# A planned attention and MLP kernel: chunk 1 of the first four heads is loaded ahead of the first two v blocks

## The chip, the core and the metric

The kernel runs on one core of a Trainium2 chip. The core has five instruction queues that run side by side and wait for each other through semaphores: TensorE (PE in the profile; its weight loads are shown apart as PEld), VectorE (DVE), ScalarE (ACT), GpSimd (POOL) and SyncE (SP). Sixteen DMA engines move data between HBM and the on-chip memories; a transfer is issued by an instruction on POOL, SP or ACT. The metric is the device time of one launch in microseconds (us). Four runs of the kernel before gave 226.29 to 227.66 us with a median of 226.47 us.

## The reference

Two layers follow each other. The first is windowed attention with sinks, for 4 sequences (b), 8 heads (h), 768 tokens, head size 64: a token sees the 128 tokens up to itself and the first 4 tokens of its sequence.

```python
scores = scale * np.matmul(q, k.transpose(0, 1, 3, 2))
keep = is_sink | in_window          # is_sink: pos < 4; in_window: 0 <= rel < 128
scores = np.where(keep, scores, -1000000000.0)
a = np.exp(scores - max); a = a / sum
attn = np.matmul(a, v)
```

The second layer takes the heads side by side as rows x of 512 numbers:

```python
xn = (x - mu) / np.sqrt(var + 1e-06) * g_ln
out = x + np.maximum(xn @ w_ch1, 0.0) @ w_ch2    # w_ch1 512x2048, w_ch2 2048x512
```

Inputs and output are float32; the kernel computes in bf16 with float32 sums.

## The kernel before, in words

**Tiles.** The 3072 tokens are 24 tiles of 128 tokens, six for each sequence. For a tile t = 6b + r, `scores` (line 567 adds a mask by a matmul with the identity for the first three tiles, line 571 is the product k times q) writes into one of two double PSUM buffers, "wide", and ACT takes the exponential (line 582). Scores of a tile come in two halves of four heads each. `values` (lines 631, 638 and 641) multiplies with v and, in a 65th column of ones, sums; then DVE divides and normalises in a chain of five instructions: reciprocal (663), multiply into xt (665), statistics (671, 674) and xn (679). The first ten tiles' xn is turned on PE (718) and copied back into xnt on ACT or DVE (copies have line 222 on ACT and 224 on DVE). `up` (742) multiplies xnt with w_ch1, ACT or DVE apply the maximum (751, 753), `down` (782) multiplies with w_ch2, DVE adds x (795) and SP stores.

**q and k.** They must have the head size on the partitions. For sequence 0 the tokens are loaded in two chunks of 384: `load_first` loads chunk 0 of heads 0 to 3 as float32 through ACT's and SP's queues and casts it on ACT and DVE; `load_runs` loads the rest through POOL with a cast on the way (192 KB each for four heads: chunk 0 of heads 4 to 7, chunk 1 of heads 0 to 3, chunk 1 of heads 4 to 7). `prep_runs` turns a chunk of two heads at a time, a "pair" (12 matmuls at line 454), and copies the result into qkt. Scores of tile 2 need both chunks, as does everything behind them; tiles 0 and 1 need chunk 0 alone. `load_v` (404) loads one block of 128 tokens of v, `load_w` (417, 420) a quarter of a weight matrix (512 KB). `sinks` prepares the four sink tokens: `sel` (303) picks them out of v by a matmul (517), `hmask` and `smask` mask them, line 530 multiplies them with q, line 535 takes the exponential into `es`.

**The order of the work** is written out by a planner, `Plan.emit`. Each piece is an `op` with a cost for an engine that can do it, the ops that it depends on, and a key; the planner walks through an estimated time line and puts the ready op with the lowest key next. Loads on POOL keep the order in which they are declared; each has an estimate, `took`, of how long its data takes after those in front of it. Up to the time `HOLD[0]` (line 46) the planner may keep an engine idle for up to `HOLD[1]` us when an op with a lower key becomes ready soon. Where it expects PE idle during the first 26 us it puts in matmuls on a constant (`spin`, line 236), whose results nobody reads. Only the order that comes out, and the real waits for data and buffers, are in the program; the estimates are not.

Of the kernel before, what the change touches and what calls it, by code (L numbers as in the profile page):

```python
# [11 lines left out]
ALU = mybir.AluOpType  # L12
# [19 lines left out]
class Plan:  # L32
# [10 lines left out]
    WARM = 26.0  # L43
    AHEAD = 2.5
    EARLY = 16.0
    HOLD = 22.0, 0.5

    def __init__(self, spin):
        self.ops, self.spin = [], spin
# [1 line left out]
    def op(self, engs, fn, deps=(), key=0.0, alloc=(), uses=(), lat=0.0):  # L51
        o = Op(engs, fn, deps, key, alloc, uses)
        o.lat = lat
        self.ops.append(o)
        return o

    def emit(self):
# [54 lines left out]
        while waiting:  # L112
# [21 lines left out]
            s, e, o, c = min((x for x in cand if x[1] == e0 and x[0] <= lim), key=lambda x: (x[2].key, x[0]))  # L134
            if s < self.HOLD[0]:

                s, e, o, c = min((x for x in cand if x[1] == e0 and (x[2] is o or x[2].key < o.key - 0.05 and
                                  x[0] < min(s + c - 0.12, s + self.HOLD[1]))), key=lambda x: (x[2].key, x[0]))
            if e == "PE" and s < self.WARM and 7 not in tenant:
# [24 lines left out]
def kernel(  # L164
# [12 lines left out]
    nc = tc.nc  # L177

    B, H, S, D = q.shape
    NS = int(n_sink)  # L180
# [7 lines left out]
    HP = H // 2  # L188
# [31 lines left out]
    def copy(e, dst, src):  # L220
        if e == "ACT":
            nc.scalar.copy(dst, src)
        else:
            ENG[e].tensor_copy(dst, src)
# [14 lines left out]
    op = plan.op  # L239
# [21 lines left out]
    spinner = consts.tile([128, 128], BF16)  # L261
# [3 lines left out]
    sel = consts.tile([128, 128], BF16)  # L265
# [24 lines left out]
    def const_negs(_):  # L290
        nc.vector.tensor_scalar(neg1, mask1, 30000.0, -30000.0, op0=ALU.mult, op1=ALU.add)
        for m1, m0, keep in ((neg1, neg0, 0.0), (mask1, mask0, 1.0)):
            nc.vector.tensor_copy(m0, m1)
            nc.vector.memset(m0[0:NS, :], keep)

    def const_sinks(_):

        nc.gpsimd.affine_select(out=hmask[:, 0:1], in_=spinner[:, 0:1], compare_op=ALU.is_ge,
                                fill=0.0, base=63, pattern=[[0, 1]], channel_multiplier=-1)
        nc.gpsimd.affine_select(out=hmask[:, 1:2], in_=spinner[:, 0:1], compare_op=ALU.is_ge,  # L300
                                fill=0.0, base=-64, pattern=[[0, 1]], channel_multiplier=1)

        nc.gpsimd.affine_select(out=sel, in_=spinner, compare_op=ALU.is_equal, fill=0.0, base=0,
                                pattern=[[0, 32], [-1, NS]], channel_multiplier=1)

        nc.gpsimd.affine_select(out=smask, in_=spinner[:, 0:H], compare_op=ALU.is_ge, fill=0.0, base=0,
                                pattern=[[-32, HP], [-4, 2]], channel_multiplier=1)
        nc.gpsimd.affine_select(out=smask, in_=smask, compare_op=ALU.is_ge, fill=0.0, base=NS - 1,
                                pattern=[[32, HP], [4, 2]], channel_multiplier=-1)
# [5 lines left out]
    begun = op({"POOL": 0.7}, None, key=-1000)  # L315
    ones_done = op({"DVE": 2.0}, None, key=-1000)
    ident_done = op({"POOL": 0.35}, const_ident, [begun], -500)
    half_masks = op({"POOL": 0.6}, const_masks, [begun], -499.5)
    masks_done = neg_done = op({"DVE": 1.3}, const_negs, [half_masks], -700)
    sinks_done = op({"POOL": 1.4}, const_sinks, [begun], -440)  # L320

# [4 lines left out]
    def load(cost, took, go, key, deps=(), alloc=(), uses=()):  # L328
        o = op({"POOL": cost}, go, [begun, issued[-1], landed[-QUEUE]] + list(deps), key, alloc, uses)
        issued.append(o)  # L330
        landed.append(op({"DMA": took}, None, [o], key))
        return landed[-1]
# [7 lines left out]
    def qn_buf(b, x):  # L340
        if (b, x) in qn:
            return []
        qn[(b, x)] = Buf("qkn", 4)
        return [qn[(b, x)]]

    def load_runs(b, c, x, h0, h1, took, key):
        alloc = qn_buf(b, x)
        qb = qn[(b, x)]
        w = S // CHUNKS[b]

        def go(_):
            if qb.t is None:
                qb.t = qkn.tile([128, H * S * D // 128], BF16, name="qkn")
            dst = qb.t.rearrange("p (c h m) -> p c h m", c=CHUNKS[b], h=H)
            nc.gpsimd.dma_start(dst[:, c, h0:h1], (q, k)[x][b, h0:h1, c * w:(c + 1) * w, :]
                                .rearrange("h (p r) d -> p h (r d)", p=128))

        o = load(0.9 if h1 - h0 == H else 0.77, took, go, key, (), alloc, [qb])
        for h in range(h0, h1):
            loaded[(b, c, x, h)] = o  # L360

    def load_first(x, hp, lands, key):

        alloc = qn_buf(0, x)
        qb, raw = qn[(0, x)], Buf("ot", 3) if x else Buf("xnt", 3)
        w = S // CHUNKS[0]

        def go(_):
            if x:
                raw.t = opool.tile([128, DM], FP32, name="ot")  # L370
            else:
                raw.t = xtpool.tile([128, NDM, 512], BF16, name="xnt").rearrange("p j c -> p (j c)").bitcast(FP32)
            (nc.scalar, nc.sync)[x].dma_start(raw.t[:, 0:w].rearrange("p (h m) -> p h m", h=2),
                                      (q, k)[x][0, 2 * hp:2 * hp + 2, 0:w, :].rearrange("h (p r) d -> p h (r d)", p=128))

        def cast(e):
            if qb.t is None:
                qb.t = qkn.tile([128, H * S * D // 128], BF16, name="qkn")
            copy(e, qb.t[:, w * hp:w * (hp + 1)], raw.t[:, 0:w])

        op({"SP": 0.1}, go, [], key, [raw])
        o = op({"XD": 0.1}, None, [], key, lat=lands - 0.8)
        o = op({"ACT": 0.49, "DVE": 0.45}, cast, [o], -600, alloc, [raw, qb])
        for h in (2 * hp, 2 * hp + 1):
            loaded[(0, 0, x, h)] = o
# [16 lines left out]
    def load_v(b, r, key, deps=(), took=0.85):  # L402
        def go(_):
            nc.gpsimd.dma_start(vn_buf[b % 2][:, r, :, 0:D],  # L404
                                v[b, :, 128 * r:128 * (r + 1), :].rearrange("h p d -> p h d"))

        before = [vread[(b - 2, i)] for i in (r, r + 1) if (b - 2, i) in vread] + [vs_done.get(b - 2)]
        vcast[(b, r)] = load(0.9, took, go, key, list(deps) + before)
# [2 lines left out]
    w2s = consts.tile([128, NH1, DM], BF16)  # L411
    w_in = {}

    def load_w(which, c, key):
        def go(_):
            if which == 1:
                nc.gpsimd.dma_start(w1s[:, :, 512 * c:512 * (c + 1)],
                                    moe_w_ch1.rearrange("(j p) c -> p j c", p=128)[:, :, 512 * c:512 * (c + 1)])
            else:
                nc.gpsimd.dma_start(w2s[:, 4 * c:4 * (c + 1), :],  # L420
                                    moe_w_ch2.rearrange("(t p) n -> p t n", p=128)[:, 4 * c:4 * (c + 1), :])

        w_in[(which, c)] = load(0.85, 2.57, go, key)


    prepped, kqb, turns = {}, {}, {}
# [393 lines left out]
        nc.tensor.matmul(gp.t, lhsT=ones, rhs=grow, start=True, stop=True)  # L820

    for x in range(2):
        load_runs(0, 0, x, HP, H, (2.2, 1.1)[x], -499)
    for n, (x, hp) in enumerate((x, hp) for hp in range(2) for x in (1, 0)):
        load_first(x, hp, (3.3, 3.5, 4.6, 4.6)[n], -1000 + n)
    op({"SP": 0.1}, lambda _: nc.sync.dma_start(grow, moe_g_ln.rearrange("(o d) -> o d", o=1)), [], -900)
    for r in range(2):
        load_v(0, r, -496 + r, took=1.4)
    for half in range(2):
        for x in range(2):  # L830
            load_runs(0, 1, x, 4 * half, 4 * half + 4, ((1.5, 1.0), (1.8, 0.6))[half][x], -490 + 2 * half + x)
    for c in range(4):
        load_w(1, c, -470 + 2 * c)
        load_v(0, 2 + c, -469 + 2 * c)
    for c in range(3):
        load_w(2, c, -440 + c)
    for x in range(2):
        load_runs(1, 0, x, 0, H, 3.85, -436 + x)
    load_w(2, 3, -434)
    for r in range(RB):  # L840
        load_v(1, r, -430 + r)
# [94 lines left out]
```

## Time and profile before

The profiled execution took 226.39 us, of which the span from the first to the last instruction is 224.7 us.

| part of the span | what it holds | PE busy |
|---|---|---|
| 0 to 5 us | loads, constants, 30 spins | 3.38 of 5.00 |
| 5 to 10 us | chunk 0 turned, first scores | 5.00 of 5.00 (13 spins and more within) |
| 10 to 15 us | scores and values of tiles 0 and 1 | 4.90 of 5.00 |
| 15 to 21.3 us | chunk 1 turned, tiles 0 and 1 normalised, scores of tile 2 | 5.50 of 6.30 |
| 21.3 to 200 us | `up`, `down`, the other tiles | all but 0.35 us |

The transfers on POOL's queue land in the order of their issue. "Lands" is the issue's start plus the time to landing of that issue:

| transfer | issued at | to landing | lands at |
|---|---|---|---|
| chunk 0, heads 4-7, q | 1.89 | 5.9 | 7.8 |
| chunk 0, heads 4-7, k | 2.90 | 5.9 | 8.8 |
| v block 0 | 3.64 | 6.0 | 9.6 |
| chunk 1, heads 0-3, q | 5.38 | 6.2 | 11.6 |
| chunk 1, heads 0-3, k | 6.12 | 6.4 | 12.5 |
| chunk 1, heads 4-7, q | 6.85 | 6.8 | 13.7 |
| chunk 1, heads 4-7, k | 7.58 | 7.3 | 14.9 |
| w_ch1, first quarter | 8.31 | 8.9 | 17.2 |
| v block 2 | 9.10 | 9.0 | 18.1 |
| w_ch1, second quarter | 11.30 | 9.3 | 20.6 |
| w_ch1, third quarter | 12.95 | 11.1 | 24.1 |
| w_ch1, last quarter | 14.56 | 12.9 | 27.5 |

In the timeline an instruction stands with its start, its duration, engine, line, operation, output and input, and a count; in square brackets is the time that its engine was idle before it, and what ended that. In the chain of work that ended last each line is a start, a duration, an engine and a line. PE's matmuls overlap by a little: the time from start to start is what one costs.

### The profile page before, as it was taken

How to read it: one execution, taken by the hardware profiler on the slowest of the kernel's cores; microseconds unless marked ns; L12 is line 12 of the kernel's file. 1: busy time of each engine (PE TensorE's matmuls, PEld its weight loads, DVE VectorE, ACT ScalarE, POOL GpSimd, SP SyncE). 2: the span in 40 equal slices, each digit the busy share in tenths (PEclk: the TensorE clock that was granted, in tenths of full speed). 3: DMA queues.
4: the chain of work that ended last, by engine and by line, in shares of the span. 5: the costliest groups of instructions: out<-in, count | busy, mean ns of one | idle time of the engine just before them, and what ended most of it. 6: DMA issues, size and time to landing. Idle time of an engine off the chain costs nothing.

```text
span 224.7 us, 4469 instructions
## 1 busy us (share of the span) xinstructions
PE 218.6 (97%) x1835; PEld 123.6 (55%) x1835; DVE 114.9 (51%) x217; ACT 111.1 (49%) x158; POOL 82.4 (37%) x111
## 2 busy tenths in 40 slices
PE   7999999999999999999999999999999999999994
PEld 6465888985545455455454444544454554444852
DVE  4565868044977879589574467470026750021011
ACT  3678775677432585870327762246613157400620
POOL 8978776668520699450733000220006020000000
PEclk9999999999999999999999999999999999999999
DMA  6999999999999599999799011230012130012102
GB/s 164 163 195 196 192 207 204 204 157 155 134 124 254 135 150 139 145 139 181 92 172 240 7 25 47 81 108 0 0 36 85 47 96 1 0 47 93 50 0 93
DMA packets 84774, 25.59 MB, mean 114 GB/s; under 512 B 74385, under 2 KB 81809, under 8 KB 84754
## 3 DMA queue, kind: packets, MB, share of 16 engines
q0 software_dynamic: 59392, 13.24, 69.2%
q1 hardware_dynamic: 24818, 11.67, 26.0%
q10 hardware_dynamic: 544, 0.39, 0.5%
q8 instruction: 14, 0.23, 0.4%
q14 instruction: 6, 0.05, 0.1%
HBM read 27.27 MB, written 6.29 MB: 149 GB/s over the span
## 4 chain that ended last, share of the span: by engine, by line
PE 91%; DVE 4%; DMA 2%; ACT 1%; issue 1%; DVEq 0%
PE single L782 38%; PE single L742 36%; PE wide L571 5%; PE wide L638 3%; PE wide L641 2%; DMA xnt<-in_q_dram 2%; PE wide L631 2%; PE wide L567 1%; PE wide L454 1%; PE single L718 1%; DVE st L671 1%; DVE xt L665 1%; PE single L236 1%; DVE xn L679 1%; PE single L454 1%
## 5 line engine op out<-in xcount | busy, mean ns | idle before, releaser
L742 PE MATMUL single<-xnt,w1s 128*128 128x256 bf16 (+1 forms) x512 | 87.9, 326 | 0.0
L742 PEld LDWEIGHTS <-w1s 128*128 128x128 bf16 x512 | 48.4, 98 | 32.6 <-issue 1.9
L582 ACT ACTIVATE e<-wide 128x1024 bf16<-128x1024 f32 x44 | 43.6, 1023 | 43.4 <-PE wide L571 40.9
L782 PE MATMUL single<-w2s,h1t 128*128 128x512 bf16 x256 | 58.1, 379 | 0.0
L795 DVE SCALAR_TENSOR_TENSOR ot<-single,rs,xt 128x512 f32<-128x512 f32 (+2 forms) x25 | 18.2, 728 | 60.3 <-PE single L782 45.1
L751 ACT ACTIVATE h1t<-single 128x512 bf16<-128x512 f32 x60 | 35.8, 597 | 20.9 <-PE single L742 20.9
L782 PEld LDWEIGHTS <-h1t 128*128 128x128 bf16 x256 | 24.0, 98 | 28.2 <-issue 1.1
L782 PE MATMUL single<-w2s,h1n 128*128 128x512 bf16 (+2 forms) x144 | 30.2, 356 | 0.0
L751 ACT ACTIVATE h1n<-single 128x512 bf16<-128x512 f32 x30 | 17.9, 597 | 22.4 <-PE single L742 22.2
L594 POOL TENSOR_SCALAR_AFFINE_SELECT e<-e 128x512 bf16<-128x512 bf16 (+1 forms) x10 | 7.1, 706 | 46.3 <-ACT e L582 46.3
L691 POOL TENSOR_SCALAR ve<-mv 128x2 f32<-128x2 f32 (+1 forms) x8 | 5.7, 708 | 48.0 <-DVE mv L674 48.0
L404 POOL DMA_DIRECT2D vn<-in_v_dram x24 | 21.7, 920 | 0.0
L592 DVE TENSOR_TENSOR e<-e,mask 128x1024 bf16<-128x1024 bf16 x22 | 15.9, 722 | 9.5 <-ACT e L582 9.3
L782 PEld LDWEIGHTS <-h1n 128*128 128x128 bf16 x144 | 12.6, 98 | 12.3 <-issue 1.3
L679 DVE SCALAR_TENSOR_TENSOR xn<-xt,mv,gb 128x512 bf16<-128x512 bf16 x24 | 18.3, 768 | 0.8
L671 DVE BATCH_NORM_STATS2 st<-xt 128x6 f32<-128x512 bf16 x24 | 16.7, 694 | 0.8
L665 DVE TENSOR_TENSOR xt<-wide,rc 128x512 bf16<-128x512 f32 x24 | 16.6, 691 | 0.8
L638 PE MATMUL wide<-vn,e 128*128 128x65 bf16 x192 | 15.8, 193 | 0.1
L638 PEld LDWEIGHTS <-e 128*128 128x128 bf16 x192 | 13.7, 97 | 2.6 <-issue 0.2
L571 PE MATMUL wide<-qkt 64*128 64x256 bf16 (+1 forms) x192 | 14.5, 263 | 0.0
L641 PE MATMUL wide<-vn,e 128*128 128x65 bf16 x160 | 14.2, 193 | 0.0
L571 PEld LDWEIGHTS <-qkt 64*128 64x128 bf16 x192 | 6.8, 94 | 10.3 <-issue 8.9
(66 smaller groups left out, 165.6 us busy)
## 6 DMA issues: line engine op xcount, KB each, us to landing
out_dram<-ot SPq DMA_DIRECT2D x23, 256.0 KB, 2.2
vn<-in_v_dram POOLq DMA_DIRECT2D x24, 128.0 KB, 8.1
w1s<-in_moe_w_ch_dram POOLq DMA_DIRECT2D x4, 512.0 KB, 10.2
w2s<-in_moe_w_ch_dram POOLq DMA_DIRECT2D x4, 512.0 KB, 13.3
qkn<-in_q_dram POOLq DMA_DIRECT2D x12, 128.0 KB, 8.4
qkn<-in_k_dram POOLq DMA_DIRECT2D x12, 128.0 KB, 8.2
qkn<-in_q_dram POOLq DMA_DIRECT2D x1, 768.0 KB, 14.8
qkn<-in_k_dram POOLq DMA_DIRECT2D x1, 768.0 KB, 17.9
```

The lines of the kernel that those rows point to most:

```text
L404: nc.gpsimd.dma_start(vn_buf[b % 2][:, r, :, 0:D], v[b, :, 128 * r:128 * (r + 1), :].rearrange("h p d -> p h d"))
L571: nc.tensor.matmul(pb.t[:, h2, i], lhsT=kb.t[64 * h2:64 * (h2 + 1), 1, hp, 128 * r:128 * (r + 1)], rhs=kb.t[64 * h2:64 * (h2 + 1), 0, hp, ...
L582: nc.scalar.activation(eb.t, pb.t, AF.Exp, scale=scale)
L638: nc.tensor.matmul(pv[:, half, hh, :], lhsT=weights_of(t, half, i, h2, 0), rhs=vn[:, r, h, 0:D + 1], start=fresh and hh == 0, stop=(r == 0 ...
L641: nc.tensor.matmul(pv[:, half, hh, :], lhsT=weights_of(t - 1, half, i, h2, 128), rhs=vn[:, r - 1, h, 0:D + 1], start=False, stop=True, ski ...
L665: nc.vector.tensor_tensor(xb[t].t.rearrange("p (a h) d -> p a h d", a=2), pv[:, :, :, 0:D], rc[0].unsqueeze(3).to_broadcast([128, 2, 4, D] ...
L671: nc.vector.bn_stats(st, xf)
L679: nc.vector.scalar_tensor_tensor(xnb[t].t, in0=xf, scalar=mvb[g][:, ti, 0:1], in1=gb, op0=ALU.subtract, op1=ALU.mult)
L742: nc.tensor.matmul(pb.t[:, n * i:n * (i + 1)], lhsT=w1s[:, j, 128 * (h0 + i):128 * (h0 + i + 1)], rhs=xtb[g].t[:, j, 0:n], start=(j == 0), ...
L751: nc.scalar.activation(hb.t, pb.t, AF.Relu)
L782: nc.tensor.matmul(pb.t[:, 0:n], lhsT=hidden(g, ht, ti), rhs=w2s[:, ht, c0:c1], start=(ht == 0), stop=(ht == NH1 - 1))
L795: nc.vector.scalar_tensor_tensor(ob.t[:, 0:n], in0=pb.t[:, 0:n], scalar=rsb[g][:, ti:ti + 1], in1=xb[t].t.rearrange("p h d -> p (h d)")[:, ...
```

## The change

Three things are edited. (1) The loads on POOL are declared in another order: chunk 1 of heads 0 to 3 (q, k) now stands ahead of v blocks 0 and 1, not behind them. (2) The mask `sel` is taken out of `const_sinks` into an op of its own with an early key, which puts it ahead of the first load on POOL; the other four selects keep the late key. (3) The planner gets other numbers: `HOLD[0]` is 14 and not 22, and the landing estimates of the loads up to the first quarter of w_ch1 are new.

```diff
-    HOLD = 22.0, 0.5
+    HOLD = 14.0, 0.5
...
+    def const_sel(_):
+
+        nc.gpsimd.affine_select(out=sel, in_=spinner, compare_op=ALU.is_equal, fill=0.0, base=0,
+                                pattern=[[0, 32], [-1, NS]], channel_multiplier=1)
+
     def const_sinks(_):
...
-        nc.gpsimd.affine_select(out=sel, in_=spinner, compare_op=ALU.is_equal, fill=0.0, base=0,
-                                pattern=[[0, 32], [-1, NS]], channel_multiplier=1)
...
-    sinks_done = op({"POOL": 1.4}, const_sinks, [begun], -440)
+    op({"POOL": 0.5}, const_sel, [begun], -499.4)
+    sinks_done = op({"POOL": 0.9}, const_sinks, [begun], -440)
...
-    def load_w(which, c, key):
+    def load_w(which, c, key, took=2.6):
...
-        w_in[(which, c)] = load(0.85, 2.57, go, key)
+        w_in[(which, c)] = load(0.85, took, go, key)
...
     for x in range(2):
-        load_runs(0, 0, x, HP, H, (2.2, 1.1)[x], -499)
+        load_runs(0, 0, x, HP, H, (2.1, 1.02)[x], -499)
     for n, (x, hp) in enumerate((x, hp) for hp in range(2) for x in (1, 0)):
-        load_first(x, hp, (3.3, 3.5, 4.6, 4.6)[n], -1000 + n)
+        load_first(x, hp, (3.75, 3.9, 4.75, 4.85)[n], -1000 + n)
...
-    for r in range(2):
-        load_v(0, r, -496 + r, took=1.4)
     for half in range(2):
         for x in range(2):
-            load_runs(0, 1, x, 4 * half, 4 * half + 4, ((1.5, 1.0), (1.8, 0.6))[half][x], -490 + 2 * half + x)
+            load_runs(0, 1, x, 4 * half, 4 * half + 4, ((1.1, 1.0), (1.05, 2.1))[half][x], -498 + 2 * half + x)
+        if half == 0:
+            for r in range(2):
+                load_v(0, r, -496.5 + 0.1 * r)
     for c in range(4):
-        load_w(1, c, -470 + 2 * c)
+        load_w(1, c, -470 + 2 * c, 2.6 if c else 2.25)
         load_v(0, 2 + c, -469 + 2 * c)
```

Since the planner decides the order, the edit moves instructions on other engines too. In the two built programs, with the spins left out, the order on PE, ACT and DVE differs only ahead of some 45 us of the trace before:

| engine | order before | order after |
|---|---|---|
| PE | values 0, values 1, pair 0, pair 1, turn xn 0, pair 2, pair 3, scores of tile 2 (first half) and 3 (first half), turn xn 1, 517, 530, scores of tile 2 (second half), `up` | values 0, pair 0, values 1, pair 1, pair 2, turn xn 0, pair 3, scores of tile 2 (first half) and 3 (first half), 517, turn xn 1, scores of tile 2 (second half), 530, `up` |
| ACT | copies of pairs 0 and 1, xnt 0, copies of pairs 2 and 3, xnt 1, exp of tile 2 (first half), es, exp of tile 3 (first half) | copies of pairs 0, 1 and 2, xnt 0, copy of pair 3, exp of tile 2 (first half), xnt 1, exp of tile 3 (first half), es |
| DVE | ks (503), then the two chains of five | the two chains of five, then ks |
| PE spins | 30, 13, 1, 2, 1, 2, 10, 5, 6, 7 (77) | 34, 12, 1, 1, 2, 1, 2, 2, 4, 3, 6 (68) |

("Pair" is chunk 1 of two heads here.) Behind the first `up`, everything from the turn of tile 3 to the turn of tile 5 comes one block of eight `up` matmuls earlier; PE's blocks from the turn of sequence 1 (line 454, 45.47 us) to the end come in the same order. POOL issues v block 5 and the first quarter of w_ch2 ahead of the first two tiles' variances (691), and no longer behind them; the four selects left in `const_sinks` come three loads later.

## The prediction

> **What bounds the kernel now.** I read the page first, then PE's busy time by stage, the chain of work that ended last, the timelines of PE and ACT up to 28 us, and the landing of each early load. The page's first row says that PE sets the time; the windows of the span say where it doesn't (columns: window, its length, busy us and count of PE, PEld, DVE, ACT, POOL, then clock, DMA share, GB/s):
>
> ```profile
> PE 218.6 (97%) x1835; PEld 123.6 (55%) x1835; DVE 114.9 (51%) x217; ACT 111.1 (49%) x158; POOL 82.4 (37%) x111
> ...
> 15.00:21.30 6.30, 5.50 (x79) 3.25 (x74) 3.97 (x9) 5.72 (x9) 3.89 (x6) 1.00 1.56 193
> 21.30:30.00 8.70, 8.70 (x107) 7.13 (x106) 7.29 (x15) 6.38 (x9) 7.29 (x11) 1.00 1.47 196
> 30.00:50.00 20.00, 19.65 (x279) 17.11 (x278) 8.74 (x16) 13.59 (x23) 12.09 (x15) 1.00 1.56 192
> 50.00:100.00 50.00, 50.00 (x410) 25.59 (x409) 38.00 (x72) 30.19 (x41) 28.77 (x36) 1.00 1.89 153
> ```
>
> From 21.3 us, where the first `up` begins, PE has no hole but 0.35 us, at a granted clock of 1.00. Before it, its busy time includes 77 spins and 0.80 us are empty. The useful matmuls are the same before and after, and so is their order from 45 us on. So the time moves by what the first `up` moves, less what opens behind it. The chain up to there, its steps over 0.1 us:
>
> ```profile
> 13.14 0.22 DVE rc L663
> 13.38 0.70 DVE xt L665
> 14.11 0.71 DVE st L671
> 14.84 0.19 DVE mv L674
> ...
> 15.72 0.21 DVE rc L663
> 15.96 0.70 DVE xt L665
> 16.68 0.71 DVE st L671
> 17.41 0.19 DVE mv L674
> 17.63 0.76 DVE xn L679
> ...
> 18.44 0.41 PE single L718 x4
> 18.87 0.59 ACT xnt L222
> ...
> 19.51 0.40 PE single L530 x4
> 19.91 0.50 PE single L236 x7
> ...
> 20.43 0.59 PE wide L567 x2
> ```
>
> DVE's two normalisations run from 13.14 to 18.39, one behind the other, and start when `values` of tile 0 ends. Nothing in the edit shortens that. But once the second xnt is copied, at 19.46, the first `up` could start, and it starts at 21.28: line 530, seven spins and the second half of tile 2's scores stand in front. Those scores wait for a wide buffer, which ACT gives back late. ACT's timeline:
>
> ```profile
> 14.83 1.50 ACT L222 COPY qkt<-single 128x768 bf16<-128x768 bf16 x2 [1.19 <-DVE st L671]
> 16.30 0.59 ACT L222 COPY xnt<-single 128x512 bf16<-128x512 bf16 x1
> 16.78 1.51 ACT L222 COPY qkt<-single 128x768 bf16<-128x768 bf16 x2
> 18.87 0.59 ACT L222 COPY xnt<-single 128x512 bf16<-128x512 bf16 x1 [0.58 <-PE single L718]
> 19.35 1.03 ACT L582 ACTIVATE e<-wide 128x1024 bf16<-128x1024 f32 x1
> ```
>
> ACT idles 1.19 us at 13.64, because pair 0 of chunk 1 is turned only at 14.27, and 0.58 us at 18.29. The exponential that frees the buffer ends at 20.38.
>
> **The change, part by part.** Starts below are those of the timelines.
>
> *The two loads moved ahead.* k of chunk 1, heads 0-3, lands at 12.5 us now. v blocks 0 and 1 stand ahead of it and land 0.84 and 0.9 us after their predecessors, so it comes to some 10.8, and pair 0 can be turned right behind `values` of tile 0, which ran at 12.63 to 12.87 beside ten spins (12.87, 0.72 us). Pair 0's 12 matmuls take 0.4 us (24 take 0.79 in the chain), so ACT copies it at 13.64, when its fourth exponential ends, with no idle time. In exchange v blocks 0 and 1 wait for two loads of 1.1 and 0.9 us: 9.6 becomes 11.6, 10.5 becomes 12.5. `values` of tile 0 needs the first at 12.63 and of tile 1 both at 13.69. Both are in time, by 1.0 and 1.2 us: cost nothing; without that cover each us later would delay DVE's chain by one.
>
> The Trainium skill ("DMA: Bandwidth & Descriptors", section "Anatomy of one DMA") gives one transfer on this path 2.0 us plus its bytes over 436 GB/s; for 196608 bytes an estimate of 0.45 us apiece behind a full queue, so v would be 0.9 us later rather than 2.0. The landings here are 0.9 to 1.25 us apart, and the measurement decides; by either figure v is in time, and the sum is the same.
>
> *The copies and the exponential on ACT.* Pair 0: 13.64 to 14.39 (0.75, from "1.50 x2"). Pair 1 is turned behind `values` of tile 1 (ends 14.27), done at 14.7: copy 14.75 to 15.5. Pair 2 needs the last chunk-1 load, 14.9: turned by 15.6 behind four spins, copy 15.65 to 16.4. xnt of tile 0, ready for its copy at 16.3 as now: 16.4 to 17.0. Pair 3: 17.0 to 17.75. Exponential of tile 2's first half, whose scores stand behind pair 3 on PE (done 17.75): 17.75 to 18.75. So it is over before the second xnt comes at 18.87, rather than at 20.38.
>
> *PE up to the first `up`.* The turn of xn 1 at 18.44 and its copy, 18.87 to 19.46, stay. Behind the turn (0.41): six spins (0.50, the row of 18.90) to 19.3; line 567 twice 0.53, line 571 0.32, line 530 0.33 (starts to starts, from 20.43 and 19.51): `up` at 20.5. Now 21.28: a gain of 0.75 us. The buffers are free by then: single0 from pair 3's copy, single1 and single2 from the DVE products behind 517, which need 0.76 us from 18.6 (ks, 0.19, is now in front of them) and end at 19.4.
>
> *`sel` on POOL.* It stands ahead of the first load. As issued it costs 0.47 us (10.26 to 10.73); the selects beside it at 1.13 and 1.39 cost 0.26. All eight early issues shift by 0.26 to 0.47. What reaches the landings is not in the trace: in its windows the POOL queue moved its first packets in 4.25 to 4.5 us, when the two hardware queues still had work until 5.0, and the DMA engines were never without. So the lower end is 0, and a gain is excluded because the loads in question can't be issued earlier. The upper end is 0.47. I take 0.2, the middle: while the hardware queues have the engines to themselves they finish sooner, which returns part. The k of chunk 0, heads 4-7, lands at 8.8, and PE's turn of it starts at 8.81: no slack, so scores, `values` and the chain move by these 0.2.
>
> *The other selects on POOL.* Now at 9.98, they come behind three more loads: 1.89 + 0.47 + 6.42 (eight issues) + 4.93 (w and v pairs) = 13.7 to 14.55, beside DVE's xt and st. Two ends: at 34.26 an xn took 1.16 us rather than 0.75 beside a POOL select, so 0.41; the st in front of it, beside the same select, took 0.69 as everywhere, so 0. I take 0, since xn starts at 15.05, behind them.
>
> The Trainium skill ("SBUF — State Buffer", section on the shared port) says that a DVE instruction with two SBUF inputs and a GpSimd one that reads SBUF block each other fully, and that one with a single SBUF input does not. xn has two, st one, xt one beside its PSUM input, so by the rule the sum is 0 too, as long as the selects end before xn; the rule would bring 0.4 were POOL half a us late. The row of 34.26 agrees with it.
>
> *HOLD and the estimates* cost nothing themselves. Their product is the order: first spins 34 for 30 (30 took 3.38, so 34 end at 4.95 where the turn starts at 5.00), one spin of 0.06 ahead of the turn at 8.81, which waits for its load in any case.
>
> *Behind the first `up`.* Tile 3's xn must be ready one block of eight earlier. From the end of tile 2's `values` (24.24 now) PE has 0.33 + 0.98 + 0.72 + 0.33 + 0.98 + 0.22 + 1.75 = 5.31 us to the turn; DVE starts 0.21 later and needs, without the xnt copy now done by ACT, 5.14: 5.35. Stall 0.05. `up` needs the last quarter of w_ch1 (27.5) at some 29.0, sequence 1's k (25.89 plus 17.9, 43.8) at 44.9. Both hold. SP's order is unchanged; on POOL the variances (691) now stand behind two more loads, and their first reader, the addition of x (795), comes at 59.73.
>
> **Sum.** −0.75 + 0.2 + 0.05 = −0.5 us. The profiled execution's 226.39 (span 224.7 and 1.7 around it) becomes 225.9; it lies 0.08 under the median of the runs, 226.47.
>
> **The rivals.**
>
> *Nothing comes of it.* `sel` costs the full 0.47, and DVE meets a select for 0.3: 226.4. For it: the chain has no slack at 8.8. Against: it needs both ends at once.
>
> *ACT becomes the bound through a late last load: slower.* The place is ACT between 15.6 and 18.9: pair 2, xnt, pair 3, exponential and second xnt now stand in one row with 0.1 us of slack, all behind the k of heads 4-7. Each us past 15.2 for that landing delays the first `up` by one. The gain is gone at 15.9; with 16.7 it is 227.2, and past 17.1 measurably slower. For it: its new estimate in the diff is 2.1 us where 0.6 stood. Against: the bytes ahead of it are the same, and it landed at 14.9.
>
> *The stalls behind go too: clearly faster.* PE's 0.35 us of holes between 30 and 50 us stand at 35 (for xn) and at 48 (for a copy). Were they and `sel`'s 0.2 nothing, −0.75 − 0.35 = −1.1: 225.3, or 225.2 with tile 3's xn in time too. Against: the same blocks stand around both holes.
>
> **How the numbers follow.** Forecast 0.60 (225.6 to 226.2), nothing 0.19, ACT bound 0.13 (most of it past 226.9), clearly faster 0.08. A measurement of this kernel can tell about 0.5%, 1.1 us, from no change. 225.2 is the fastest rival's time; 226.9 takes in "nothing" and the mild half of a late load; some 0.15 is left out. Below 225.3 (0.5%) I put 0.08, above 227.6 0.09.
>
> **What would show it.** First `up` at 20.5 to 20.9; ACT without a gap from 8.9 to 18.7; PE spins 68; the exponential of tile 2's first half in front of the second xnt copy; chunk 0's k at 8.8 to 9.2, v blocks 0 and 1 at 11.6 to 12.9, the last chunk-1 k at 14.9 to 15.2; PE's hole at 35 still there. I am wrong if `values` of tile 0 waits for v or starts past 13.2, or if a DMA landing ends a PE wait behind 21 us.

## The result, and the profile after

The changed kernel took 226.27 us (median of 52 runs, 225.49 to 228.30); the kernel before, on the same chip, 227.14 us (78 runs, 226.25 to 232.17). The ratio is 0.9972, with a 95% interval of 0.9962 to 0.9983: 0.3% faster, inside what was called no change. Ratios, and the counts of the last table below, leave out executions in a slower state (over 1.5% above the fastest of the same kernel), while medians and ranges hold all; the two medians alone would give 0.996. The forecast was 225.9 us, within 225.2 to 226.9. The profiled execution of the changed kernel took 227.41 us (span 225.7): it lies 1.1 us above its median, and the profile shows why.

First the page's row of busy times, which is nearly that of before, with nine matmuls fewer (the spins):

```profile
PE 219.3 (97%) x1826; PEld 123.3 (55%) x1826; DVE 115.4 (51%) x216; ACT 111.7 (49%) x159; POOL 81.3 (36%) x111
```

The windows of the span (window, length, then busy us and count of PE, PEld, DVE, ACT, POOL, then clock, DMA share, GB/s), cut at the first `up`:

```profile
15.00:20.50 5.50, 5.16 (x70) 2.81 (x69) 4.22 (x11) 5.01 (x7) 3.86 (x9) 1.00 1.57 192
20.50:30.00 9.50, 9.07 (x113) 7.09 (x110) 8.03 (x14) 7.46 (x12) 7.35 (x10) 1.00 1.48 197
30.00:50.00 20.00, 19.65 (x277) 17.08 (x275) 8.33 (x15) 13.33 (x22) 11.34 (x15) 1.00 1.54 194
50.00:100.00 50.00, 50.00 (x410) 25.48 (x408) 38.02 (x72) 30.19 (x41) 29.43 (x37) 1.00 1.86 152
100.00:150.00 50.00, 49.00 (x356) 23.82 (x355) 30.42 (x55) 19.80 (x28) 10.12 (x13) 1.00 0.78 104
```

PE now has two holes that it didn't have: 0.43 us between 20.5 and 30, and 1.00 us behind 100. The chain of work that ended last (start, duration, what) names both:

```profile
17.91 0.76 DVE xn L682
...
18.71 0.40 PE single L721 x4
19.11 0.34 PE single L236 x6
19.45 0.43 PE wide L570 x2
19.88 0.33 PE wide L574 x4
20.20 0.33 PE single L533 x4
20.53 0.98 PE single L745 x8
...
25.55 1.14 DVE xn L682
...
28.51 0.76 DVE xn L682
...
29.31 0.40 PE single L721 x4
...
115.89 1.00 issue
116.90 1.02 PE single L745 x4
```

(From the planner's loads on, a line number after is 3 higher than before: `up` is 745, the turn of xn 721, xn 682.) The first `up` starts at 20.46 in the timeline, not at 21.28. Then PE waits for the normalisation of tile 3 at 29.31, behind one of tile 2 that took 1.14 us rather than 0.75, and at 115.89 it stands for a microsecond, for which the profile names no releaser ("issue"). ACT's timeline (start, duration, engine, line, operation; in brackets the idle time before it and what ended that) shows the exponential of tile 2's first half, at 18.15, ahead of the second xnt copy, at 19.15, as forecast:

```profile
13.78 0.79 ACT L222 COPY qkt<-single 128x768 bf16<-128x768 bf16 x1
15.08 0.80 ACT L222 COPY qkt<-single 128x768 bf16<-128x768 bf16 x1 [0.50 <-DVE st L674]
16.29 0.80 ACT L222 COPY qkt<-single 128x768 bf16<-128x768 bf16 x1 [0.41 <-PE single L457]
16.98 0.59 ACT L222 COPY xnt<-single 128x512 bf16<-128x512 bf16 x1
17.46 0.82 ACT L222 COPY qkt<-single 128x768 bf16<-128x768 bf16 x1
18.15 1.05 ACT L585 ACTIVATE e<-wide 128x1024 bf16<-128x1024 f32 x1
19.15 0.59 ACT L222 COPY xnt<-single 128x512 bf16<-128x512 bf16 x1
```

**An account that holds for all kernels.** PE does the same work in all of them (but for a few spins), so four marks on PE's timeline split every profile: the second turn of chunk 0 (heads 2 and 3), the first `up`, the first turn of sequence 1 (48 matmuls at line 457, 454 before), and the end of the span.

| profile | start to 2nd turn | to first `up` | to sequence 1 | to the end | middle two |
|---|---|---|---|---|---|
| before | 6.29 | 14.99 | 24.19 | 179.23 | 39.18 |
| after | 6.36 | 14.10 | 24.87 | 180.37 | 38.97 |
| after, second profile | 6.26 | 14.08 | 24.56 | 179.80 | 38.64 |
| after, third profile | 7.02 | 14.07 | 24.48 | 179.23 | 38.55 |
| v first again | 6.27 | 14.07 | 24.48 | 179.18 | 38.55 |
| tile 3's turn later | 6.91 | 14.07 | 24.18 | 179.24 | 38.25 |
| issues rotated | 6.08 | 14.08 | 24.86 | 179.18 | 38.94 |
| `sel` back | 6.04 | 14.07 | 24.49 | 179.20 | 38.56 |
| v first, tile 3 later, one spin less | 6.55 | 13.91 | 24.61 | 179.23 | 38.52 |
| turns of tiles 11-13 early | 6.05 | 14.08 | 24.48 | 179.99 | 38.56 |
| load order alone | 6.59 | 14.63 | 23.63 | 179.95 | 38.26 |
| HOLD alone | 6.29 | 14.56 | 23.82 | 179.33 | 38.38 |
| HOLD alone, second profile | 6.22 | 14.55 | 23.47 | 179.36 | 38.02 |
| HOLD, turns of tiles 11-13 early | 6.79 | 14.55 | 23.47 | 179.19 | 38.02 |

The first and fourth columns vary from execution to execution of one kernel; the middle two agree within 0.02 us where the order of PE, ACT and DVE is the same, but for the time of one DVE instruction (below). In "load order alone" and the HOLD kernels a block of four score matmuls (0.33 us) lies ahead of the first `up` rather than behind, so their second column is to be read 0.33 lower and the third 0.33 higher. The profiled execution of after came out 1.02 us slower than that of before: +0.07 in front, −0.89 to the first `up`, +0.68 behind it, +1.14 at the end.

### The profile page after: what moved, and what is told of

Same layout as the page of the kernel before. It is cut to its first block, busy times and chain, and to the rows that moved or that the text cites. A ratio compares the mean times of both kernels' runs of the same rounds, so it can differ in the third digit from the quotient of the medians.

```text
span 225.7 us, 4452 instructions
## 1 busy us (share of the span) xinstructions
PE 219.3 (97%) x1826; PEld 123.3 (55%) x1826; DVE 115.4 (51%) x216; ACT 111.7 (49%) x159; POOL 81.3 (36%) x111
## 3 DMA queue, kind: packets, MB, share of 16 engines
HBM read 27.27 MB, written 6.29 MB: 149 GB/s over the span
## 4 chain that ended last, share of the span: by engine, by line
PE 90%; DVE 7%; issue 1%; ACT 0%; DVEq 0%
PE single L785 37%; PE single L745 34%; PE wide L574 5%; PE single L236 3%; PE wide L641 2%; PE wide L644 2%; DVE xn L682 2%; DVE st L674 2%; DVE xt L668 2%; PE wide L634 1%; PE wide L457 1%; PE wide L570 1%; PE single L721 1%; PE single L457 1%; PE single L533 1%
## 5 line engine op out<-in xcount | busy, mean ns | idle before, releaser
L694 POOL TENSOR_SCALAR ve<-mv 128x2 f32<-128x2 f32 (+1 forms) x8 | 4.6, 575 | 47.2 <-DVE mv L677 47.1
L595 DVE TENSOR_TENSOR e<-e,mask 128x1024 bf16<-128x1024 bf16 x22 | 15.9, 722 | 8.7 <-ACT e L585 8.6
```

## The experiments

Medians are of 9 to 12 runs, beside 30 to 35 runs of the kernel before on the same chip: 226.70 us for the first four, 226.76 for the second four, 226.61 for the last four.

### First four: where behind the first `up` does the time go?

**after, once more** (`e_after`, no edit).

> The changed kernel again, unaltered, as the yardstick for the others on this chip, and for a second profile. Theory: the gain is made ahead of the first `up` matmul (20.46 us in its first profile against 21.28 before), and part of it is given back at the turn of tile 3 (line 721), where PE waited from 28.7 to 29.3 for an xn that came late because the xn of tile 2 took 1.14 us and not 0.75. If that stretch comes and goes between executions, a profile without it has the turn of tile 3 by 28.9 and a span of 223.9 to 224.1; with it, 224.4 to 224.6. The 1.0 us hole of PE at 115.9, for which the profile shows no cause, should not be there again, or stand elsewhere. Ratio to the kernel before 0.996 to 0.998. Rival: the hole belongs to the change; then it stands at the same place again.

Measured: 226.30 us, ratio 0.9984 [0.9966, 1.0002]; profiled 226.4. The long xn of tile 2 did not come again (0.84 us; the turn of tile 3 at 28.89). The late hole did, 0.43 us at the same place, as the rival had it.

**v blocks first again** (`e_v_first`): the changed kernel with the two v blocks declared ahead of chunk 1. PE, ACT and DVE keep their order.

```diff
+    for r in range(2):
+        load_v(0, r, -498 + 0.1 * r)
     for half in range(2):
         for x in range(2):
-            load_runs(0, 1, x, ..., -498 + 2 * half + x)
-        if half == 0:
-            for r in range(2):
-                load_v(0, r, -496.5 + 0.1 * r)
+            load_runs(0, 1, x, ..., -497.5 + 0.5 * half + 0.1 * x)
```

> The changed kernel with v blocks 0 and 1 loaded first again, as before the change, and the planner's order on PE, ACT and DVE the same instruction for instruction. Theory: what counts is the order on PE and ACT; with v first, k of chunk 1, heads 0-3, lands by 12.5 to 13.0 us, still ahead of its turn at 13.2, so the time is that of the changed kernel within 0.2 us and the first `up` starts at 20.4 to 20.6. Rival: the new place of the loads is what pays; then the turn of pair 0 waits, `values` of tile 1 stands behind it, and the first `up` comes 0.3 to 0.8 us later, with the whole at 226.4 or above.

Measured: 225.83 us, 0.9971 [0.9955, 0.9986]; profiled 225.77. The way to the first `up` is 14.07 us with either order of the loads. Once the order of the engines stands, the order of the loads is worth nothing there. The median lies 0.47 us under that of after beside it, more than the 0.2 expected, though the middle two columns are those of after's third profile; the intervals overlap, and this profile has no hole at 116.

**Tile 3's turn one block later** (`e_turn3_later`): the planner is told that tile 3's xn is ready 0.6 us later, so it puts the turn behind one more block of eight `up` matmuls, as before the change. In the built program that tile's xnt copy also goes from ACT to DVE.

```diff
-        o = op({"DVE": 0.75}, cen, [o, gb_done], key, [xnb[t]], [xb[t]])
+        o = op({"DVE": 0.75}, cen, [o, gb_done], key, [xnb[t]], [xb[t]], 0.6 if t == 3 else 0.0)
```

> The changed kernel with tile 3's turn planned 0.6 us later, so that it stands behind one more block of eight `up` matmuls, as before the change; nothing else of PE's order differs but that values of tile 4 follow the turn directly. Theory: PE does not wait there, and the sequence from 29 us on comes 0.2 us earlier where tile 2's xn takes 0.75 us and 0.5 us earlier where it takes 1.14; the median is 0.2 to 0.5 us below the changed kernel's. Rival: what is won there is lost again at the turn of sequence 1 (line 457), whose k landed at 44.7 and whose turn began at 45.3; then at most 0.6 us can be kept, and a PE wait for that load appears; or tile 4's turn, one chain of DVE further, takes over the wait, and the time is the changed kernel's within 0.1 us.

Measured: 226.14 us, 0.9976 [0.9955, 0.9997]; profiled 226.09. PE's timelines from the turn of tile 2 (line 721) on, first of after:

```profile
26.98 1.91 PE L745 MATMUL single<-xnt,w1s 128*128 128x256 bf16 x16
29.31 0.40 PE L721 MATMUL single<-ident,xn 128*128 128x128 bf16 x4 [0.43 <-DVE xn L682]
```

of the kernel with v first:

```profile
26.78 1.91 PE L745 MATMUL single<-xnt,w1s 128*128 128x256 bf16 x16
28.80 0.40 PE L721 MATMUL single<-ident,xn 128*128 128x128 bf16 x4
```

and with the turn later:

```profile
27.41 2.78 PE L745 MATMUL single<-xnt,w1s 128*128 128x256 bf16 x24
30.04 0.39 PE L721 MATMUL single<-ident,xn 128*128 128x128 bf16 x4
```

Start to start, sixteen `up` matmuls should take two thirds of the 2.63 us of the last fence, 1.75. In after they take 2.33 up to the turn, so 0.58 are lost; with v first 2.02, so 0.27, though this timeline marks no idle time there; with the turn later nothing. The column "to sequence 1" falls from 24.48 to 24.18 by about this. The medians are 0.16 us apart, which is within the scatter of single runs.

**The issues on POOL rotated** (`e_rotate`): in the place of a quarter of w_ch2 stands sequence 1's q, in its place sequence 1's k, in that of k the quarter.

```diff
+    three = [o for o in plan.ops if o.key in (-438, -436, -435) and "POOL" in o.engs]
+    third, q_of_1, k_of_1 = [o.fn for o in three]
+    three[0].fn, three[1].fn, three[2].fn = q_of_1, k_of_1, third
```

> The changed kernel with three issues on POOL rotated: sequence 1's q is issued where the third quarter of w_ch2 was, its k where its q was, and the quarter of w_ch2 where the k was, beside tile 2's xn; nothing else differs. Theory: it is the issue of that k (25.42 to 26.29) that stretched tile 2's xn from 0.75 to 1.14 us; with the other issue there xn takes 0.75 and the time falls by 0.2 to 0.4 us. Rival: any issue on POOL does it, or something that comes and goes between executions; then xn stays at 1.14 in this profile too, or the medians agree within 0.1 us.

Measured: 225.96 us, 0.9967 [0.9955, 0.9979]; profiled 225.95. The theory that the issue of sequence 1's k in particular stretches tile 2's xn fell: here the issue at 25.09 is that of w_ch2, and xn takes 1.14 us as in after. The median is 0.34 us under after's all the same: medians of twelve differ by this much without the account showing why, so the readings here rest on its columns. What the long xn have in common is the start of an issue on POOL just ahead of them. One stretch of the timeline of all engines in after:

```profile
25.42 0.87 POOL L358 DMA_DIRECT2D qkn<-in_k_dram  x1 [0.23 <-issue]
...
25.55 1.14 DVE L682 SCALAR_TENSOR_TENSOR xn<-xt,mv,gb 128x512 bf16<-128x512 bf16 x1
...
26.30 0.88 POOL L597 TENSOR_SCALAR_AFFINE_SELECT e<-e 128x512 bf16<-128x512 bf16 x1
```

and with v first:

```profile
25.06 0.89 POOL L358 DMA_DIRECT2D qkn<-in_k_dram  x1
...
25.42 0.75 DVE L682 SCALAR_TENSOR_TENSOR xn<-xt,mv,gb 128x512 bf16<-128x512 bf16 x1
...
25.93 0.72 POOL L597 TENSOR_SCALAR_AFFINE_SELECT e<-e 128x512 bf16<-128x512 bf16 x1
```

The select that follows on POOL is the obvious rival, but it starts while xn still runs in both. Its time less the stretch that it shares with xn is 0.49 us in after (0.88 less 0.39) and 0.48 here (0.72 less 0.24). So it looks as if the select waits for xn, and not xn for the select.

### Second four: which part of the edit brings the gain?

**The load order alone** (`e_loads`): the kernel before with only the declaration moved; estimates, HOLD and `sel` as they were.

```diff
-    for r in range(2):
-        load_v(0, r, -496 + r, took=1.4)
     for half in range(2):
         for x in range(2):
-            load_runs(0, 1, x, ..., -490 + 2 * half + x)
+            load_runs(0, 1, x, ..., -498 + 2 * half + x)
+        if half == 0:
+            for r in range(2):
+                load_v(0, r, -496.5 + 0.1 * r, took=1.4)
```

> The kernel before with nothing but the loads' new order; HOLD, the estimates and `sel` stay. The planner then turns pair 0 right behind values of tile 0, but keeps the second xnt copy on ACT ahead of tile 2's exponential. Theory: the gain belongs to the planner's numbers, and the loads' new place only makes every later landing 0.5 to 1 us later (the last chunk-1 k landed at 14.9 to 15.9 in three profiles with the new order against 14.9 before and 14.5 with v first); so no gain: 226.3 to 226.8, ratio to the kernel before 0.999 to 1.001. Rival, the title of the change: turning pair 0 early is what pays, and the ratio is 0.998 or below.

Measured: 225.63 us, 0.9956 [0.9938, 0.9975]; profiled 226.51, with a hole of 0.59 us at 116. The rival's number came in, not the theory's. But that pair 0's early turn is what pays doesn't follow: the theory had the order wrong, and here too the exponential of tile 2 no longer waits behind the second xnt copy, which DVE does (at 19.26 us; the exponential goes out at 18.48).

**HOLD alone** (`e_hold`): the kernel before with one number changed.

```diff
-    HOLD = 22.0, 0.5
+    HOLD = 14.0, 0.5
```

> The kernel before with HOLD[0] at 14 and nothing else. In the order that comes out line 530 stands ahead of tile 2's second half and both second halves (tiles 2 and 3) stand ahead of the first `up`, which then runs two blocks at once. Theory: a part of the gain, since the pairs of chunk 1 are still turned where they were and ACT still idles at 13.6: ratio 0.998 to 1.000. Rival 1: HOLD alone is the whole gain, 0.9975 or below. Rival 2: without the new estimates the order fits the chip worse and it is slower, above 1.001.

Measured: 225.57 us, 0.9952 [0.9935, 0.9970]; profiled 225.68: rival 1. Run once more in the third comparison (`e_hold_again`):

> The kernel before with HOLD[0] at 14 alone, once more, beside the changed kernel on the same chip. If that single number is worth what it seemed to be (0.9952 of the kernel before, 225.6): 225.4 to 225.8, 0.3 us or more under the unaltered changed kernel. If the difference of 0.7 us was one of the chips: 226.0 to 226.4, with intervals that overlap fully.

Measured: 225.73 us, 0.9967 [0.9942, 0.9992]; profiled 225.34. This is 0.49 us under after's 226.22 beside it, as the first theory had it, though the intervals overlap in part. ACT's timeline of this second profile:

```profile
14.77 1.50 ACT L222 COPY qkt<-single 128x768 bf16<-128x768 bf16 x2 [1.20 <-DVE st L671]
16.23 0.58 ACT L222 COPY xnt<-single 128x512 bf16<-128x512 bf16 x1
16.72 1.51 ACT L222 COPY qkt<-single 128x768 bf16<-128x768 bf16 x2
18.10 1.97 ACT L582 ACTIVATE e<-wide 128x1024 bf16<-128x1024 f32 x2
```

The 1.20 us of idle time are still there, since the loads are in the old order; but the exponential goes out at 18.10 all the same. HOLD had kept ACT idle for the second xnt copy (0.58 us before); that copy is now done by DVE, in 0.42. So most of the gain ahead of the first `up` needs neither the loads nor pair 0's early turn. From `values` of tile 0 to the first `up` it is 8.65 us before, 7.88 here (8.21 less the block of 0.33 that comes early), 7.95 with the load order alone (8.28 less 0.33) and 7.59 after. The further 0.3 us of after lie behind the turn of xn 1 (1.75 us to the first `up`, 2.07 with HOLD alone by the same reckoning): line 517 no longer stands there, and fewer spins. And this order loses another hole. PE's timeline ahead of tile 4's turn:

```profile
30.75 2.79 PE L742 MATMUL single<-xnt,w1s 128*128 128x256 bf16 x24
33.38 0.39 PE L718 MATMUL single<-ident,xn 128*128 128x128 bf16 x4
```

24 matmuls take 2.63 us start to start here, and 2.90 before and after (32.57 to 35.47 before). There xn of tile 4 takes 1.16 us beside a select on POOL, here 0.75.

Either part alone shortens the middle two columns more (38.02 to 38.38) than the whole change does (38.55 to 38.97). They don't add up: in the built programs, with the loads moved and the estimates and `sel` as before, HOLD at 14 or at 22 gives the same order on every engine. What after has on top of that, new estimates and `sel` early, turns that order into the one with the stall at tile 3; which of the two does it was not run.

**`sel` back behind the loads** (`e_sel_moved`): in the changed kernel the instruction alone goes back; its place in the plan stays, empty.

```diff
-    op({"POOL": 0.5}, const_sel, [begun], -499.4)
-    sinks_done = op({"POOL": 0.9}, const_sinks, [begun], -440)
+    op({"POOL": 0.5}, None, [begun], -499.4)
+    sinks_done = op({"POOL": 0.9}, lambda e: (const_sel(e), const_sinks(e)), [begun], -440)
```

> The changed kernel with the instruction that makes `sel` back behind the loads on POOL, 0.47 us later on, and everything else in the same order. As the prediction had it, its early place delays the first transfers and with them the chain by 0.2 us: then PE's turn of chunk 0, heads 4-7, starts 0.2 us sooner, at 8.8, and the time falls by 0.2. What the profiles after say against it: that load lands at 7.6 to 7.8 and its turn starts at 8.96 to 9.06, so it isn't waited for, and what moved the turn is one spin in front of it and the turns before; then the turn stays at 8.9 to 9.1 and the time within 0.1 us.

Measured: 226.18 us, 0.9963 [0.9942, 0.9984]; profiled 225.5. The turn starts at 8.74, but that is 2.70 us behind the second turn, as in after; this execution was early from the start (6.04). The middle takes 38.56 us, as in the undisturbed profile of after (38.55): `sel`'s place costs nothing there.

**Three remedies at once** (`e_best_spin`): v first, tile 3's turn later, and no single spin ahead of the turn of chunk 0, heads 4 to 7.

```diff
-                for _ in range(n):
+                for _ in range(0 if n == 1 and 7.0 < s < 9.0 else n):
```

> The changed kernel with v blocks 0 and 1 loaded first, with tile 3's turn one block of eight later, and without the single spin ahead of the turn of chunk 0, heads 4-7. Theory: the three terms add. The spin moves the chain by 0.15 us (turn at 8.8, values of tile 0 at 12.6, first `up` at 20.2), the turn of tile 3 is not waited for, and from the first `up` to the turn of sequence 1 PE needs 24.2 us, as before the change, so that this starts at 44.4; its k must land by then (44.1 with v first). Median 225.4 to 225.7, ratio 0.995 to 0.997. Rivals: the k of sequence 1 lands after 44.4, PE waits there, and the time is that of the version with v first; or the block at 115 us waits for tiles turned through the DMA, which start no sooner, and takes the gain back.

Measured: 226.03 us, 0.9957 [0.9942, 0.9972]; profiled 226.03. The spin brings 0.16 us (13.91 for 14.07), but xn of tile 4 took 1.37 us in this profile, and PE waited 0.32 us for it, where it waited 0.11 with tile 3's turn later alone. So in this profile what was won at tile 3 was lost at tile 4. The median missed its 225.4 to 225.7 and lies between those of the parts (225.83 and 226.14); the ratio lies inside what was expected, and its interval overlaps theirs. That the three terms add is not shown.

### Last four: the hole at 116 us

Three of the ten profiles so far had it: after, its second, and the load order alone. The first `up` of tiles 10 to 13 follows it. These tiles are turned by DMA, and SP issues the last three behind twelve transposes of sequence 3's token blocks. SP's timeline in after:

```profile
88.41 18.67 SPq L481 DMA_TRANSPOSE qkt<-qkn  x12
107.17 4.89 SPq L711 DMA_TRANSPOSE xnt<-xn  x3
```

The list of DMA issues (the last number is the time from issue to landing) gives for the third of them, issued at 110.8 us in after:

```profile
xnt<-xn SPq DMA_TRANSPOSE x1, 6.0
```

It lands at 116.8, and `up` starts at 116.90. In the second profile of after it is 115.8 (`up` at 115.90), in the load order alone 115.9 (116.01): some 0.1 us ahead of `up` each time. In six of the seven profiles without a hole it lands at 112.8 to 114.5, over 0.8 us ahead of `up`; in HOLD alone it is 115.1 (115.16), just late enough to cost that profile some 0.1 us in the last column. To test it, the three turns were issued ahead of the last two token blocks, in the changed kernel and in the one with HOLD alone; nothing else moves.

```diff
+    KEYS = 18.86, 26.4, 38.7, 45.68
+    slots = [o for o in plan.ops if "SP" in o.engs and any(abs(o.key - k) < 0.001 for k in KEYS)]
+    slots.sort(key=lambda o: o.key)
+    fns = [o.fn for o in slots]
+    for o, fn in zip(slots, fns[2:] + fns[:2]):
+        o.fn = fn
```

> The changed kernel unaltered, beside the three others of this comparison. Theory A (what is left of the change's gain is lost around 115 us: the first `up` of tiles 10 to 13 waits for tile 13's turn, which SyncE issues behind twelve others): 226.1 to 226.5, and a hole of 0.4 to 1.0 us in PE at some 116 us. Theory B (the hole is an accident of single executions, the gain is lost ahead of 45 us): the same median, and mostly no hole.

> The changed kernel; on SyncE alone the turns of tiles 11, 12 and 13 are issued ahead of the last two of sequence 3's twelve token blocks and no longer behind them, everything else is the same. Tile 13's turn is then issued 3.1 us earlier (two transfers of 1.55 us) and lands by some 113 us. Theory A: no hole at 116 us, PE's start of the block of 48 turns to the end of the span takes 179.2 us as in the kernels without a hole, and the median is 0.4 to 0.8 us under the unaltered changed kernel's. Theory B: within 0.2 us of it.

> The kernel before with HOLD[0] at 14, and the turns of tiles 11 to 13 issued ahead of the last two token blocks of sequence 3 on SyncE. Theory A: this kernel's profile had no hole at 116 us, so 0 to 0.2 us under it, 225.3 to 225.6, and fewer executions above 226. Theory B: the same as it.

| kernel | median (range), us | runs over 0.5 above the median | ratio |
|---|---|---|---|
| after | 226.22 (225.55 to 230.31) | 2 of 11 | 0.9981 [0.9961, 1.0002] |
| after, turns early | 226.05 (225.52 to 226.51) | 0 of 12 | 0.9970 [0.9955, 0.9985] |
| HOLD alone | 225.73 (225.21 to 228.07) | 2 of 12 | 0.9967 [0.9942, 0.9992] |
| HOLD, turns early | 225.67 (224.90 to 225.94) | 0 of 10 | 0.9944 [0.9925, 0.9963] |

Neither theory is quite right. The hole is real and is the turn's landing as far as the landings show, but only some executions have it: the third profile of after has none. With the turns issued early no run lies far above its median (0 of 22, against 4 of 23), which are few runs to go by; the medians moved by 0.17 and 0.06 us, which is theory B's number and less than theory A's 0.4 to 0.8 for the changed kernel. After with the turns early has another hole in its profile; SP's timeline:

```profile
87.51 16.54 SPq L481 DMA_TRANSPOSE qkt<-qkn  x10
104.14 4.97 SPq L711 DMA_TRANSPOSE xnt<-xn  x3
109.20 2.53 SPq L481 DMA_TRANSPOSE qkt<-qkn  x2
111.86 0.49 SPq L803 DMA_DIRECT2D out_dram<-ot  x1
```

The two token blocks now stand ahead of an output store. DVE's next product for the output waits for a store to land, and PE waits for DVE:

```profile
118.27 0.75 DVE L798 SCALAR_TENSOR_TENSOR ot<-single,rs,xt 128x512 f32<-128x512 f32 x1 [2.82 <-DMA out_dram<-ot]
```

```profile
119.08 2.75 PE L745 MATMUL single<-xnt,w1s 128*128 128x512 bf16 x12 [0.60 <-DVE ot L798]
```

That the edit opened this hole is not shown. In the first two profiles of after DVE waits for a store at the same place (2.17 and 1.52 us) without holding up PE, and HOLD with the turns early, where SP has the same edit, has no such wait.

The kernel with HOLD at 14 and the turns early has the lowest ratio of all: 0.9944 of the kernel before, and 225.67 us beside 226.22 for the changed one, while it keeps the old load order. Its interval just touches that of the changed kernel.

## Why the prediction was right, point by point

The time was right: −0.5 us forecast, 0.3% or some 0.6 us measured by the ratio. The medians alone would not have told: 226.27 is 0.37 us above the forecast and nearer to the 226.4 of the rival "nothing comes of it". The kernel before came out at 227.14 here, not at the 226.47 that the forecast started from.

That the sum came out is in part luck. In the third profile of after, which has neither the long xn of tile 2 nor the late hole, the account reads −0.92 to the first `up` and +0.29 behind it: −0.63. The gain is larger than forecast by 0.3, the stall at tile 3 by 0.2, and these two errors nearly cancel; the 0.2 put down to `sel` came from a spin.

- **PE up to the first `up`, forecast −0.75.** The mechanism was right (the exponential ahead of the second xnt copy), the size 0.3 us too small. From `values` of tile 0 to the first `up` it was 8.65 us before and is 7.59 after: −1.06. The step that failed is "behind the turn (0.41): six spins (0.50)". Those are durations, and on PE the next group starts before a row has ended; from start to start the turn costs 0.24 and the six spins 0.33. That is 0.34 us given away.
- **Why the exponential comes first** was put down to the loads: pair 0 turned early, ACT "without a gap". ACT still has gaps of 0.50 and 0.41 us, and HOLD alone gets the exponential to 18.10 with the loads in the old order. "HOLD and the estimates cost nothing themselves; their product is the order" was right in words, but the product of HOLD alone was never worked out. Alone it brings 0.77 of the 1.06 us, and the load order alone 0.70.
- **`sel`, forecast +0.2.** The mechanism fell. Chunk 0's k landed at 7.8 us, earlier than before (8.8), and moving `sel` back changes nothing. The step "one spin of 0.06 ahead of the turn at 8.81, which waits for its load in any case" failed: the turn doesn't wait for its load, and the spin costs 0.17 (second turn to third: 2.52 before, 2.70 after).
- **Tile 3's stall, forecast 0.05.** Measured 0.28 undisturbed, 0.58 in the first profile. Of the 0.23 too few, 0.11 come from PE's terms (two blocks of `up` at 0.98 take 0.88, `values` at 0.72 takes 0.81), some 0.13 from DVE's chain (PE's turn starts 5.48 us after the end of `values`, not 5.35). The other 0.30 are the long xn of tile 2, which no step named.
- **The other selects, forecast 0 "since xn starts at 15.05, behind them".** The reason failed, the size held. POOL waited 0.71 and 0.25 us for landings ahead of two later loads, which the sum left out, and ran the four selects from 14.78 to 15.56. xn of tile 0 started beside them at 15.30 and took 0.78 us for 0.75.
- **v in time by 1.0 and 1.2 us.** It held, but barely in the first profile: 12.8 and 13.6 us, for `values` at 12.87 and 13.93. In others the first lands at 11.1 to 12.4.
- **The rival "ACT bound by a late last load".** The load did land at 15.9 us, where the gain was to be gone, and the turn of pair 2 waited 0.24 us for it. The first `up` came at 20.46 all the same. The slack is at least 0.7 us, not 0.1.
- **The rival "the stalls behind go too"** did not come in after, where the hole at 35 us stands as forecast, but in the kernel with HOLD alone: 2.63 us for 2.90.
- **"I am wrong if a DMA landing ends a PE wait behind 21 us."** By the landings this happened, at 116 us, in the profiled execution: by its own sign the prediction failed there. Three of the first ten profiles have this hole, and issuing the turns early moved the median by 0.17 us, so little of the forecast hangs on it.
- **"0.80 us are empty"** ahead of the first `up` is the window from 15 us alone. From the start PE is idle for 2.52 us; no term of the sum rests on it.

## What to carry to other kernels

Where the rows of an engine overlap, as PE's do here, cost a step from start to start, never by the duration of its row. When a change has several parts and a planner between the edit and the program, build each part alone and read its order first: here each of two parts alone gives what the whole gives, as far as the ratios can tell, and one constant does it without moving a load. Before a single profile is explained, split it at marks that all variants share; what varies between executions of one kernel then stands in columns of its own.

## What the hardware showed that was not expected

**The first microseconds vary.** The second turn of chunk 0 starts at 6.04 to 7.02 us, and in the profiles of one and the same kernel at 6.26, 6.36 and 7.02. No load is late in the last: it is PE's speed. PE's timeline in the third profile of after:

```profile
4.85 0.85 PE L457 MATMUL single<-ident,qkn 128*64 128x128 bf16 x12
5.63 1.46 PE L236 MATMUL single<-spinner 128*128 128x128 bf16 x12
7.02 0.53 PE L457 MATMUL single<-ident,qkn 128*64 128x128 bf16 x12
```

and with the issues rotated:

```profile
4.85 0.53 PE L457 MATMUL single<-ident,qkn 128*64 128x128 bf16 x12
5.31 0.84 PE L236 MATMUL single<-spinner 128*128 128x128 bf16 x12
6.08 0.53 PE L457 MATMUL single<-ident,qkn 128*64 128x128 bf16 x12
```

The same twelve spins take 1.39 us from start to start in one and 0.77 in the other, the twelve matmuls of the first turn 0.78 and 0.46, though the profile gives a granted clock of 1.00 for both. The Trainium skill ("TensorE: Matmul & The Clock Gate", section "Part 1: The HAM clock gate (the "warmup" mystery)") says that PE starts at half rate until it has been busy for a window of some 3.4 us, and that this window runs freely, so that the number of slow matmuls differs from run to run of one kernel. That agrees with these rows, where the slow phase ends near 5 us or past 6.5; that it is the cause was not tested. Between the earliest and the latest second turn lies 0.98 us (0.76 within the one kernel), more than the 0.6 us that the whole edit brings.

**An xn beside a starting DMA issue.** xn of tile 2 took 1.14 us where POOL began to issue a DMA 0.13 or 0.14 us ahead of it (after, issues rotated), 0.84 at 0.36 us (second profile), and 0.75 at 0.36 or 0.37 us in five others (v first among them) and at 0.47 (before). The select behind the issue waits for xn in all of these: its time less the stretch beside xn is 0.48 or 0.49 us. With HOLD alone xn once took 1.49, beside two selects of which the first began 0.32 us ahead of it. The Trainium skill ("SBUF — State Buffer", section "Who interferes with whom") says that a VectorE instruction with two SBUF inputs, as xn is, contends with a GpSimd instruction that reads SBUF, not with one that only writes; it infers that generating a DMA's descriptors needs the write interface. By that an issue would not hold up xn; the rows here suggest that it can. Which part of the issue does it, and why 0.36 us came out both ways, stays open, and no run isolates the issue.
